# Half of a first layer by seven chained half-size products, with its sums, orders and stores rearranged

## The chip, the core and the metric

The kernel runs on one core of a Trainium2 chip. The core has TensorE (PE in the profile: matrix products into PSUM, with weight loads as PEld), VectorE (DVE), ScalarE (ACT), GpSimd (POOL), and DMA queues that are issued from SyncE (SP), ScalarE or GpSimd. Each engine works through its own instructions in the order in which the program lists them, and waits where an operand of another engine isn't there yet. SBUF is the working memory, PSUM the small memory that only TensorE accumulates in and that ScalarE and VectorE read and write; this kernel uses it as four pairs of banks, each pair 128 partitions x 2 x 448 floats. The metric is the time of one execution on the device in microseconds (us). The profile is one such execution, recorded by the hardware; its span runs from the first to the last instruction.

## What is computed

An attention with normalised q and k, 8 batches of 12 heads, 448 tokens and 64 dimensions, and behind it two layers over 3584 tokens (d_model 768, d_ff 2048) with a gelu between them:

```python
q_n, k_n = rmsnorm(q, g_q), rmsnorm(k, g_k)
attn = softmax(q_n @ k_n^T / sqrt(64))
x = (attn @ v) as 3584 tokens x 768
h = x @ w_in                                  # 768 x 2048
g = 0.5*h*(1 + tanh(sqrt(2/pi)*(h + 0.044715*h**3)))
out = g @ w_out                               # 2048 x 768
```

## The kernel before

The order of every engine's work is written out by hand (a manual schedule). For batch b the kernel runs `attention(b)` (line 584) and then the first layer of b, in the loop at line 1009. Inside `attention(b)` TensorE interleaves, by the strings `STEADY` and `SECOND`, the scores of 21 units (`unit`), the row sums and products with v (`products`), and the second layer of the batch before (`quartered`). ScalarE does the exps; VectorE adds the exps up (steps A, B, F, G), transposes and inverts the sums (`turned`, `recip`, `spread`: T, R, S) and writes x, transposed, as `xT[b]` (`quad_x`: M).

The **first layer** of b multiplies the six 128-row chunks of `xT[b]` (448 tokens wide) with `win`, 2048 columns in 16 blocks of 128. Two blocks make one PSUM pair, so there are eight pairs, and behind each ScalarE writes `g` by one gelu of 128 x 896. From batch 1 on each product is cut into quarters of 64 x 64 (`mm1_turn`, line 523, products at line 537): four of them, on different quarters of the array, make one 128x128 product. Chunks 4 and 5 of x come last from the attention; so the first pairs are begun with chunks 0 to 3 (`early`, at the end of `attention`) and finished in the loop at line 1076 (`late`).

Beside the first layer of b, by the entries of `m1` (step of the loop, action), run: on GpSimd the normalisation of the next batch's q and k (`normed_both`, three chunks, line 278) and some squares for the batch after that (`square`), held back at first by a small copy that waits for VectorE (`gpsimd_waits`); on SP's queue the transposing DMAs of the normalised q and k (`transposed`) and loads for the batch after (`loads`); on ScalarE the other half squares (`squared`, line 162); on VectorE their sums (`total`, line 173) and the gain of k (`gain`, line 325), which waits for the transposing DMA. Entries under "first" in `extra` come at the start of the next attention.

The **second layer** works with two batches' `g` side by side. Only its last 512 tokens, behind batch 7, are done in `final` (line 728) by seven products of half size (Strassen's scheme in Winograd's form, TensorE at line 754), from sums of `w_out` (`weight_sum`, line 717) and of tokens of `g` (`token_sums`, lines 723 to 726) that VectorE makes beside batch 7's first layer. `put_out` stores results by two DMAs for each piece, both from SP's queue, but for the very last pieces, where ScalarE's queue takes one of the two.

The PSUM pairs are handed out in turn by `pair`. Buffers: `xT` has two, `ex` (exps of a chunk, 128 x 6272 bf16) two, the stage results `st` and `rb` of VectorE one each.

Of the kernel before, what the change touches and what calls it, by code (L numbers as in the profile page):

```python
# [17 lines left out]
def kernel(  # L18
# [38 lines left out]
    xp = ctx.enter_context(tc.tile_pool(name="xp", bufs=2))  # L57
# [346 lines left out]
    def spread(rs=slice(0, 2), rc=None):  # L404
        m = S // 32
        if rs.start == 0:
            oas["rb"] = stp.tile([128, 2, S], F32, tag="rb", name="rb")
# [159 lines left out]

    early, late = range(HP - 2), range(HP - 2, HP)
# [15 lines left out]
    def attention(b, side, extra, ends):  # L584
# [94 lines left out]
        mm1_turn(b, 0, 0, early, begin=True)  # L679
        mm1_turn(b, 1, 0, early, begin=True)  # L680
        mm1_turn(b, 0, 1, early)
        if b == 1:
            mm1_turn(b, 2, 0, early, begin=True)
        mm1_turn(b, 1, 1, early)
        if b == 1:
            mm1_turn(b, 2, 1, early)
# [10 lines left out]
    def sums_homes():  # L697

        two = exq.tile([P, 2 * NJ, HD], BF16, tag="ex", name="tw")
        one = exq.tile([P, NJ, HD], BF16, tag="ex", name="tw")  # L700
        sw.update({3: two[:, :NJ], 2: two[:, NJ:], 4: one})
        sw[1] = w4[:, :, 0, HD:]

        def home(t):
            return t[:, :NJ * TH].rearrange("p (j s) -> p j s", j=NJ)

        sa[1] = g4[:, :, 0, late2]
        sa[2] = home(kT.rearrange("p c t r s -> p (c t r s)"))
        sa[3] = home(vb[0].rearrange("p h t d -> p (h t d)"))
        sa[4] = home(vb[1].rearrange("p h t d -> p (h t d)"))  # L710

    def weight_sum(i):
# [3 lines left out]
        x, y = {3: (b12, b22), 2: (b11, sw[3]), 4: (b21, sw[2]), 1: (b12, b11)}[i]  # L716
        nc.vector.tensor_sub(sw[i], x, y)
# [10 lines left out]
    def final(b):  # L728

        token_sums(slice(NJ - 2, NJ))  # L730
        tiles = [[op.tile([128, d_model], F32, tag="osb", name="osb") for _ in range(2)]]
# [6 lines left out]
        def operands(i, j, t):  # L738
# [4 lines left out]
            if i == 4:  # L743
                return g4[:, j, 1, late2.start + lo:late2.start + lo + 128], sw[4][:, j]
# [24 lines left out]
        for t in range(2):  # L769
# [13 lines left out]
            for lo in (0, HD // 2):  # L783
                cols = slice(HD + lo, HD + lo + HD // 2)
                add(c1[:, cols], product(3, t, lo, lo + HD // 2), c1[:, cols])
                put_out(t, 0, cols, (nc.sync, nc.scalar))
# [222 lines left out]
    for b in range(B):  # L1009
        m1, side, extra, ends = [], [], [], []  # L1010
        if b == 0:
# [10 lines left out]
            extra += [("first", lambda: late_loads(2, 0)), ("L0", lambda: late_transposed(1, 2)),  # L1022
# [15 lines left out]
        elif b + 1 < B:  # L1038

            m1.append((0, lambda: gpsimd_waits(ess[b, NCH - 1][:1, 0, 0, :1])))  # L1040
            if b == 1:
                halves = [(n, slice(a, a + 1)) for n in "qk" for a in range(2)]
                m1 += [(0, lambda n=n, hs=hs: square(2, 1, n, nc.gpsimd, hs)) for n, hs in halves]
                m1 += [(0, lambda n=n, hs=hs: total(2, 1, n, hs)) for n, hs in halves]
                m1 += [(0, lambda n=n: total(2, 2, n)) for n in "qk"]
                m1.append((0, lambda: rsqrt_last(2, slice(1, NCH))))
            for c in range(NCH):
                m1 += [(0, lambda c=c: normed_both(b + 1, c, nc.gpsimd)),
                       (4 * c + 4, lambda c=c: turns_and_loads() if (b, c) == (1, 1)
                        else transposed(b + 1, c))]  # L1050
            m1.append((9, lambda: gain(b + 1, 0)))
            if b == 1:
                extra.append(("first", lambda: gain(2, 1)))
            else:
                m1.append((14, lambda: gain(b + 1, 1)))
        if 0 < b and b + 2 < B:
            m1.append((4, lambda: loads(b + 2, 1)))
            if b > 1:
                m1.append((8, lambda: loads(b + 2, 2)))
            for c, at in ((0, 4), (1, 9)):  # L1060
                for i, (n, a) in enumerate((n, a) for n in "qk" for a in range(2)):
                    m1.append((at + i, lambda c=c, n=n, a=a: squared(b + 2, c, n, a)))
                m1 += [(at + 2, lambda c=c: total(b + 2, c, "q")),
                       (at + 4, lambda c=c: total(b + 2, c, "k"))]
            for n in "qk":
                m1.append((13, lambda n=n: square(b + 2, 2, n, nc.gpsimd)))
                extra.append(("first", lambda n=n: total(b + 2, 2, n)))
        if 0 < b and b + 1 < B:
            extra.append(("first", lambda: gain(b + 1, 2)))
        if b + 1 == B:  # L1070
            m1.append((4, sums_homes))
            m1 += [(f, lambda i=i: weight_sum(i)) for f, i in ((4, 3), (6, 2), (8, 4), (10, 1))]
            m1 += [(f, lambda js=js: token_sums(js))
                   for f, js in ((7, slice(0, 4)), (11, slice(4, 6)))]
        m1 = plan(*m1)
        for f in range(nf // 2 if b == 0 else nf):
# [72 lines left out]
```

## Time and profile before

| | us |
|---|---|
| median of 3 runs | 389.36 (388.61 to 389.49) |
| the profiled execution | 389.53 |
| its span | 387.8 |
| first layers of batches 1 to 7 (line 537), busy | 128.7 |
| second layers (line 495), busy | 152.0 |
| scores (line 335), busy | 59.9 |
| exps on ScalarE (line 343), busy | 156.1 |
| gelus on ScalarE (line 543), busy | 50.5 |
| seven products at the end (line 754), 128 of TensorE's instructions | 364.7 to 383.1 |

Times in the trace count from the start of the span. A row of a timeline gives start, duration, engine, line, operation, written tile <- read tiles, shape, the number of instructions merged into it (x33), and in brackets how long the engine was idle before and for whom it waited. A row of the groups gives, behind the count, the busy time in us and the mean of one instruction in ns, then the idle time before. A row of the chain gives start, duration and what. Recorded products on TensorE overlap: the next one starts before the end of the one before, so the distance of their starts is what a product costs.

### The profile page before, as it was taken

The numbers are of one execution on the slowest core, as the hardware profiler recorded it, in microseconds if no ns is written. First come the engines' busy times: TensorE is split into PE (matmuls) and PEld (weight loads), VectorE is DVE, ScalarE is ACT, GpSimd is POOL, SyncE is SP. The second block draws the span as 40 slices with busy tenths as digits, with TensorE's granted clock in tenths as the row PEclk, the third lists the DMA queues.
The fourth block names the chain that finished last, engine by engine and source line by source line (L and its number), as shares of the span: only waits on it lengthen the run. The fifth ranks groups of instructions, "written<-read, shape, count | busy, mean of one in ns | idle before, by whom it ended". The sixth has DMA issues, their size and how long they took to land.

```text
span 387.8 us, 17506 instructions
## 1 busy us (share of the span) xinstructions
PE 379.0 (98%) x8020; PEld 294.2 (76%) x8020; DVE 259.9 (67%) x394; ACT 276.6 (71%) x348; POOL 126.0 (33%) x109
## 2 busy tenths in 40 slices
PE   8899999999999999999999999999999999999995
PEld 5565586679888788877888778877888778887653
DVE  5998949984896259835589156963588503895743
ACT  6995599677994689757996589946897449953400
POOL 5996504448105440083102740064400810000000
PEclk9999999999999999999999999999999999999999
DMA  8999999979914992369822995159823630220033
GB/s 274 318 232 210 210 227 230 263 176 181 222 44 99 258 199 55 85 139 224 176 73 64 181 257 110 45 111 235 111 61 82 109 59 19 69 64 5 2 79 83
DMA packets 65085, 54.66 MB, mean 141 GB/s; under 512 B 37748, under 2 KB 61172, under 8 KB 65012
## 3 DMA queue, kind: packets, MB, share of 16 engines
q1 hardware_dynamic: 54576, 41.43, 44.5%
q0 software_dynamic: 10128, 11.80, 18.4%
q8 instruction: 62, 1.02, 1.0%
q10 hardware_dynamic: 308, 0.33, 0.3%
q14 instruction: 11, 0.09, 0.1%
HBM read 45.61 MB, written 11.01 MB: 146 GB/s over the span
## 4 chain that ended last, share of the span: by engine, by line
PE 92%; ACT 5%; DMA 1%; issue 1%; DVE 0%; POOL 0%
PE t L537 33%; PE t L495 32%; PE t L387 9%; PE t L335 8%; PE t L754 5%; ACT ex L343 4%; PE t L556 4%; DMA rawq<-in_q_dram 1%; PE h L436 1%; PE tp L296 1%; PE o L387 0%; POOL nrmq L278 0%; DVE ss L173 0%; ACT sq L162 0%; PE os L387 0%
## 5 line engine op out<-in xcount | busy, mean ns | idle before, releaser
L343 ACT ACTIVATE ex<-t,shift 128x896 bf16<-128x896 f32 x168 | 156.1, 1012 | 3.0 <-PE t L335 2.6
L495 PE MATMUL t<-wout,g 64*64 64x384 bf16 (+1 forms) x3456 | 152.0, 305 | 0.0
L495 PEld LDWEIGHTS <-g 64*64 64x64 bf16 x3456 | 115.4, 107 | 17.6 <-issue 0.2
L537 PE MATMUL t<-xT,win 64*64 64x448 bf16 x2688 | 128.7, 349 | 0.0
L537 PEld LDWEIGHTS <-win 64*64 64x64 bf16 x2688 | 98.0, 107 | 29.2
L543 ACT ACTIVATE g<-t 128x896 bf16<-128x896 f32 x56 | 50.5, 915 | 56.8 <-PE t L537 56.7
L173 DVE TENSOR_REDUCE ss<-sq 128x14 f32<-128x896 f32 (+3 forms) x45 | 44.3, 998 | 49.4 <-ACT sq L162 47.0
L335 PE MATMUL t<-qT,kT 64*64 64x448 bf16 x672 | 59.9, 351 | 1.5 <-ACT ex L343 0.6
L876 POOL COPY mark<-es 1x1 bf16<-1x1 bf16 x7 | 1.2, 177 | 134.8 <-DVE es L362 126.4
L355 DVE TENSOR_TENSOR es<-ex 128x1792 bf16<-128x1792 bf16 x21 | 22.3, 1061 | 28.9 <-ACT ex L343 28.9
L278 POOL TENSOR_TENSOR nrmq<-rawq,rinv 128x896 bf16<-128x896 f32 (+1 forms) x21 | 34.8, 1658 | 19.5 <-ACT rinv L205 10.5
L278 POOL TENSOR_TENSOR nrmk<-rawk,rinv 128x896 bf16<-128x896 f32 (+1 forms) x21 | 34.6, 1647 | 0.0
L387 PE MATMUL t<-ex,vb 64*64 64x448 bf16 x588 | 32.4, 350 | 0.5 <-issue 0.5
L335 PEld LDWEIGHTS <-kT 64*64 64x64 bf16 x672 | 26.2, 106 | 8.0 <-issue 1.9
L397 DVE STREAM_TRANSPOSE st<-t 128x448 f32<-128x448 f32 x42 | 24.7, 627 | 9.6 <-PE t L387 9.6
L387 PEld LDWEIGHTS <-vb 64*64 64x64 bf16 x672 | 23.2, 107 | 8.6 <-issue 2.1
L409 DVE STREAM_TRANSPOSE rb<-rc 128x896 f32<-128x896 f32 (+1 forms) x25 | 26.7, 1068 | 0.3
L422 DVE TENSOR_TENSOR xT<-t,rb 128x896 bf16<-128x896 f32 x21 | 22.8, 1086 | 0.9 <-PE t L387 0.2
L513 ACT COPY osb<-t 128x768 f32<-128x768 f32 (+1 forms) x18 | 12.6, 701 | 14.0 <-PE t L495 14.0
L358 DVE TENSOR_TENSOR es<-es,ex 128x1792 bf16<-128x1792 bf16 x21 | 22.3, 1062 | 0.0
L164 POOL TENSOR_TENSOR sq<-rawq 128x896 f32<-128x896 f32 (+1 forms) x9 | 13.6, 1510 | 24.3 <-DVE ss L173 11.6
L325 DVE TENSOR_SCALAR kT<-kT,gcols 128x896 bf16<-128x896 bf16 x19 | 12.1, 639 | 11.2 <-DMA kT<-nrmk 11.2
(122 smaller groups left out, 322.5 us busy)
## 6 DMA issues: line engine op xcount, KB each, us to landing
rawq<-in_q_dram SPq DMA_DIRECT2D x22, 448.0 KB, 4.6
rawk<-in_k_dram SPq DMA_DIRECT2D x22, 448.0 KB, 6.3
out_dram<-osb SPq DMA_DIRECT2D x36, 192.0 KB, 2.8
vb<-in_v_dram POOLq DMA_DIRECT2D x6, 672.0 KB, 8.1
out_dram<-osb SPq DMA_DIRECT2D x38, 96.0 KB, 2.2
win<-in_moe_w_in_dram POOLq DMA_DIRECT2D x8, 384.0 KB, 10.4
wout<-in_moe_w_out_dram POOLq DMA_DIRECT2D x3, 768.0 KB, 17.2
vb<-in_v_dram POOLq DMA_DIRECT2D x2, 448.0 KB, 15.2
```

The lines of the kernel that those rows point to most:

```text
L173: nc.vector.reduce_sum(sss[b][:, seat(b, c), "qk".index(n), hs, ts], squares(b, c, n, hs, ts), axis=AX.X)
L278: eng.tensor_mul(nrms[n, b, c][:, ts].rearrange("p t a d -> p a t d"), raws[n, b, c][:, :, ts], root[:, :, ts].to_broadcast([P, 2, m, D]),)
L335: nc.tensor.matmul(sc[r * R:(r + 1) * R, a, :S], kT[rs, c, t, r], qT[b][rs, c, :, r], start=True, stop=True,)
L343: nc.scalar.activation(exs[b, c][:, t], scs.pop((b, c, t))[:, :, :S], AF.Exp, scale=scale, bias=shift)
L355: nc.vector.tensor_add(es, ex[:, :2], ex[:, 2:4])
L387: nc.tensor.matmul(o[r][a * D:(a + 1) * D], vb[b % 2][rs, 2 * c + a, i] if what else ones[rs], es[i][rs, a], start=(i == 0), stop=(i == n ...
L397: nc.vector.transpose(st[:, r].rearrange("p a b -> p (a b)"), o[r])
L409: nc.vector.transpose(oas["rb"][:, rs].rearrange("p r s -> p (r s)"), rc.to_broadcast([128, (rs.stop - rs.start) * m, 32]),)
L422: nc.vector.tensor_mul(xT[b][:, 2 * c:2 * c + 2], oas["o", c, 1][:, :, :S], oas["rb"])
L495: mm = nc.tensor.matmul(o[a * R:(a + 1) * R, bank, :hi - lo], g[rs, f, at:at + R], wout[rs, f, lo:hi], start=(n == 0), stop=(n == len(step ...
L537: mm = nc.tensor.matmul(h[a * R:(a + 1) * R, j, :S], win[rs, c, at:at + R], xT[b][rs, c], start=begin and c == cs[0], stop=end and c == cs ...
L543: nc.scalar.activation(g[:, 2 * i:2 * i + 2, (b % 2) * S:(b % 2 + 1) * S], h[:, :, :S], AF.Gelu_apprx_tanh,)
```

## The change

For batches 2 to 7 the first layer is written anew (class `Seven`). Blocks 4 to 7 and 12 to 15 of d_ff (pairs 2, 3, 6 and 7, `LONE`) are multiplied in whole 128x128 products of 448 columns. Blocks 0 to 3 and 8 to 11 (two halves of 512 columns of `win`), chunks 0, 2, 4 against 1, 3, 5, and the two halves of the tokens (224 each) are the quadrants of Strassen's scheme: seven products, each of 4 blocks x 3 chunks in whole 128x128 products of 224 columns. They are chained in three PSUM pairs: X takes products 1, 6, 7 and 4 one upon the other, Z products 5 and 3, Y product 2. ScalarE copies X to SBUF (`keep`) after 1, after 6 and after 7, and VectorE adds the copies to Y and Z. VectorE makes four sums of x (`x_sums`, 128 x 672 bf16) in each batch. The sums of `win` are made once: three at the start of attention 1 (`in_sums`, into a new tile `wx`), one in place at the start of attention 2.

```diff
+    FS, QS = 4, S // 2
+    wv = win.rearrange("p (m k) f -> p k m f", k=2)
+    wx = wts.tile([128, 3, NCH, FS * 128], BF16, name="wx")
+    fs1, fs2 = slice(0, FS * 128), slice(d_ff // 2, d_ff // 2 + FS * 128)
+    LONE = (2, 3, 6, 7)
+    def in_sums():
+        a11, a21, a12, a22 = wv[:, 0, :, fs1], wv[:, 0, :, fs2], wv[:, 1, :, fs1], wv[:, 1, :, fs2]
+        nc.vector.tensor_sub(wx[:, 1], a21, a11)
+        nc.vector.tensor_add(wx[:, 0], wx[:, 1], a22)
+        nc.vector.tensor_sub(wx[:, 2], a12, wx[:, 0])
+    def in_place_sum():
+        a21 = wv[:, 0, :, fs2]
+        nc.vector.tensor_add(a21, a21, wv[:, 1, :, fs2])
+    class Seven:
...
+            self.rhs = {1: b11, 2: b21, 3: b22, 4: xs[:, 3], 5: xs[:, 2], 6: xs[:, 1], 7: xs[:, 0]}
+            self.lhs = {1: wv[:, 0, :, fs1], 2: wv[:, 1, :, fs1], 4: wv[:, 1, :, fs2],
+                        5: wv[:, 0, :, fs2], 6: wx[:, 0], 7: wx[:, 1], 3: wx[:, 2]}
+        def x_sums(self):
+            b11, b12, b21, b22 = self.given
+            xs, sub = self.xs, nc.vector.tensor_sub
+            sub(xs[:, 0], b12, b22)
+            sub(xs[:, 1], b11, xs[:, 0])
+            sub(xs[:, 2], b12, b11)
+            sub(xs[:, 3], b21, xs[:, 1])
...
+        def keep(self, n):
+            nc.scalar.copy(self.snaps[n], self.of("X"))
...
+        def early(self):
+            hs1.clear()
+            two = range(NCH - 1)
+            self.lone(LONE[0], range(2), early)
+            self.product(1, "X", two)
+            self.product(2, "Y", two)
+        def rest(self, steps):
...
+            self.x_sums()
+            side(0)
+            product(1, "X", one)
+            self.keep(0)
+            product(2, "Y", one)
+            add(self.of("Y"), self.of("Y"), self.snaps[0])
+            lone(LONE[0], range(2), late, end=True)
+            side(1)
+            product(6, "X")
+            self.keep(1)
+            self.gelu(self.of("Y"), 0, 0)
+            side(2)
+            product(5, "Z")
+            side(5)
+            product(7, "X")
+            self.keep(0)
+            add(self.snaps[0], self.of("Z"), self.snaps[0])
+            side(8)
+            lone(LONE[1], ones_, all_of)
+            self.gelu(self.snaps[0], 1, 1)
+            product(4, "X")
+            self.gelu(self.of("X"), 1, 0)
+            side(11)
+            product(3, "Z")
+            add(self.of("Z"), self.of("Z"), self.snaps[1])
+            self.gelu(self.of("Z"), 0, 1)
+            lone(LONE[1], twos, all_of, end=True)
+            side(15)
+            lone(LONE[2], range(2), all_of, end=True)
+            side(17)
+            lone(LONE[3], range(2), all_of, end=True)
```

The work beside the first layers of batches 2 to 6 gets new places (`side(n)` runs the entries of step n). GpSimd normalises chunk 0, then waits for the last sum of x, then goes on. ScalarE keeps six of the eight half squares, GpSimd takes the other two as one whole:

```diff
+            m1 += [(0, lambda: gpsimd_waits(ess[b, NCH - 1][:1, 0, 0, :1])),
+                   (0, lambda: normed_both(b + 1, 0, nc.gpsimd)),
+                   (0, lambda: gpsimd_waits(sevens[b].xs[:1, 3, 0, :1])),
+                   (0, lambda: normed_both(b + 1, 1, nc.gpsimd)),
+                   (0, lambda: normed_both(b + 1, 2, nc.gpsimd)),
+                   (2, lambda: transposed(b + 1, 0)), (8, lambda: transposed(b + 1, 1)),
+                   (11, lambda: transposed(b + 1, 2))]
+            if b + 2 < B:
+                m1 += [(0, lambda n=n, a=a: squared(b + 2, 0, n, a))
+                       for n in "qk" for a in range(2)]
+                m1 += [(2, lambda: loads(b + 2, 1)), (8, lambda: loads(b + 2, 2))]
+                m1 += [(5, lambda n=n: total(b + 2, 0, n)) for n in "qk"]
+                m1 += [(15, lambda a=a: squared(b + 2, 1, "q", a)) for a in range(2)]
+                m1.append((15, lambda: square(b + 2, 1, "k", nc.gpsimd)))
+                m1 += [(17, lambda n=n: total(b + 2, 1, n)) for n in "qk"]
...
+            m1 += [(5, lambda: gain(b + 1, 0)), (17, lambda: gain(b + 1, 1))]
             extra.append(("first", lambda: gain(b + 1, 2)))
+            m1 += [(5, sums_homes), (5, lambda: weight_sum(3)), (5, lambda: weight_sum(2)),
+                   (11, lambda: weight_sum(4)), (17, lambda: token_sums(slice(2, 6))),
+                   (17, lambda: token_sums(slice(0, 2)))]
```

Memory for it: `xT` has one buffer, `rb` shares that of `st`, the sums of x and the two copies of X lie in a buffer of `ex`, and one sum of `w_out` moves to two buffers of the raw q and k. At the end, the last sum of `w_out` (`weight_sum(1)`) is made in `final` behind the last token sums, and the stores are joined: a row of tiles goes out whole, half from SP's queue and half from ScalarE's, and so does the very last half row:

```diff
             add(c2[:, last], p5, c2[:, first])
             add(c1[:, last], p5, c1[:, last])
-            put_out(t, 1, last)
             add(c2[:, first], product(4, t), c2[:, first])
-            put_out(t, 1, first)
+            put_out(t, 1, slice(0, d_model), (nc.sync, nc.scalar))
...
                 add(c1[:, cols], product(3, t, lo, lo + HD // 2), c1[:, cols])
-                put_out(t, 0, cols, (nc.sync, nc.scalar))
+            put_out(t, 0, last, (nc.sync, nc.scalar))
```

More of the change, by code (lines that the diff above doesn't have):

```diff
@@ L568 @@
+    sevens = {}
     early, late = range(HP - 2), range(HP - 2, HP)
@@ L678, in attention @@
                 square(2, NCH - 1, m, nc.scalar)
[L679 to L682, printed above, removed]
+        if b > 1:
+            sevens[b] = Seven(b)
+            sevens[b].early()
+        else:
+            mm1_turn(b, 0, 0, early, begin=True)
+            mm1_turn(b, 1, 0, early, begin=True)
+            mm1_turn(b, 0, 1, early)
             mm1_turn(b, 2, 0, early, begin=True)
-        mm1_turn(b, 1, 1, early)
-        if b == 1:
+            mm1_turn(b, 1, 1, early)
             mm1_turn(b, 2, 1, early)
@@ L1037 @@
                     (f"a{at}", lambda n=n: total(2, 0, n))]
-        elif b + 1 < B:
+        elif b == 1:
             m1.append((0, lambda: gpsimd_waits(ess[b, NCH - 1][:1, 0, 0, :1])))
[L1041 to L1046, printed above, removed]
-            for c in range(NCH):
[L1048 to L1059, printed above, removed]
+            halves = [(n, slice(a, a + 1)) for n in "qk" for a in range(2)]
+            m1 += [(0, lambda n=n, hs=hs: square(2, 1, n, nc.gpsimd, hs)) for n, hs in halves]
+            m1 += [(0, lambda n=n, hs=hs: total(2, 1, n, hs)) for n, hs in halves]
+            m1 += [(0, lambda n=n: total(2, 2, n)) for n in "qk"]
+            m1.append((0, lambda: rsqrt_last(2, slice(1, NCH))))
@@ L1068 @@
-        if 0 < b and b + 1 < B:
-            extra.append(("first", lambda: gain(b + 1, 2)))
[L1070 to L1074, printed above, removed]
+                m1.append((13, lambda n=n: square(3, 2, n, nc.gpsimd)))
+                extra.append(("first", lambda n=n: total(3, 2, n)))
@@ L1075 @@
         m1 = plan(*m1)
-        for f in range(nf // 2 if b == 0 else nf):
+        if b > 1:
+            sevens[b].rest(m1)
+        for f in range((nf // 2, nf)[b] if b < 2 else 0):
             i, part = f // 4 * 2, f % 4
```

106 lines of the change are left out of this document (95 added, 11 removed).

## The prediction

> **What bounds the kernel now.** I read the page first, then the chain of waits in order of time, then the groups of instructions with shapes kept apart, then the timeline around one first layer, and last the DMA queue at the end.
>
> ```profile
> span 387.8 us, 17506 instructions
> PE 379.0 (98%) x8020; PEld 294.2 (76%) x8020; DVE 259.9 (67%) x394; ACT 276.6 (71%) x348; POOL 126.0 (33%) x109
> PE 92%; ACT 5%; DMA 1%; issue 1%; DVE 0%; POOL 0%
> ```
>
> TensorE is busy for 98% of the span, and the chain that ended last runs 92% through it. ScalarE and VectorE have about 30% to spare, but a busy share alone doesn't say whether they are idle at the right moment. The chain of waits has the stage that the change rewrites (here in batches 3 and 7, then the last products):
>
> ```profile
> 211.07 18.16 PE t L537 x384
> 346.60 18.16 PE t L537 x384
> 364.76 18.34 PE t L754 x120
> ```
>
> A first layer of a late batch is one unbroken piece of 18.16 us. It holds 384 quarter products, four of which do the work of one whole 128x128 product: 96 whole ones at 18.16 / 96 = 0.189 us. Nothing waits in it, so work removed there is time removed, unless the new order adds waits.
>
> **The products.** How far apart do whole 128x128 products start? The timeline has all widths but the new one:
>
> ```profile
> 39.78 6.41 PE L556 MATMUL t<-xT,win 128*128 128x448 bf16 x33
> 380.31 1.46 PE L754 MATMUL t<-tw,g 128*128 128x384 bf16 x8
> 381.61 1.48 PE L754 MATMUL t<-wout,vb 128*128 128x192 bf16 x16
> L754 PE MATMUL t<-wout,vb 128*128 128x192 bf16 x16 | 1.5, 246 | 0.0
> L754 PEld LDWEIGHTS <-g 128*128 128x128 bf16 x64 | 6.1, 98 | 4.4 <-issue 0.4 <-ACT g L543 0.2
> L537 PEld LDWEIGHTS <-win 64*64 64x64 bf16 x2688 | 98.0, 107 | 29.2
> ```
>
> At 448 columns: (6.41 - 0.35) / 32 = 0.189 us, the same as four quarters. At 384: (381.61 - 380.31) / 8 = 0.1625. At 192: (1.48 - 0.246) / 15 = 0.0823. The slope is (0.1625 - 0.0823) / 192 = 0.000418 us a column, so 224 columns, which no row shows, cost 0.0823 + 32 x 0.000418 = 0.0957; the bounds are 0.0823 and, should a weight load be the limit, 0.098 (that of a whole block) or 0.107 (the longest row of loads from win); I take the line between the widths shown. New stage: half of d_ff stays ordinary, 4 pairs x 2 x 6 = 48 products of 448 columns, 48 x 0.1892 = 9.08 us. The other half is seven products of 4 blocks x 3 chunks, 84 of 224 columns (96 without Strassen), 84 x 0.0957 = 8.04 us. Together 17.12, which is **1.04 us less** than 18.16, in six batches **6.24 us**.
>
> The Trainium skill, page "TensorE: Matmul & The Clock Gate", section "LDWEIGHTS (loading the stationary operand)", puts a weight load at its columns divided by 1.2, an estimate of 107 ns for 128. By that rule the 84 products would be held to their loads, and the stage would gain almost nothing (rival C has the mechanism by rows). The trace speaks against it: products of 192 columns follow each other every 82 ns, each with a load of its own that is recorded at 98 ns, so loads overlap there.
>
> **The waits that the chain adds.** Seven products share three PSUM pairs: X collects products 1, 6, 7, 4 and is copied out by ScalarE three times on the way, Y is product 2, Z products 5 and 3. TensorE, in order, must wait for each copy before it adds to X again, and everything behind it on its queue waits too. The prices:
>
> ```profile
> 18.37 9.12 ACT ex L343 x10
> 27.54 0.38 PE t L335 x4
> 229.28 0.92 ACT L543 ACTIVATE g<-t 128x896 bf16<-128x896 f32 x1 [0.22 <-PE t L537]
> L513 ACT COPY osb<-t 128x768 f32<-128x768 f32 x12 | 9.7, 812 | 0.0
> L513 ACT COPY osb<-t 128x384 f32<-128x384 f32 x6 | 2.9, 478 | 14.0 <-PE t L495 14.0
> L774 DVE TENSOR_TENSOR osb<-t,osb 128x384 f32<-128x384 f32 x2 | 1.1, 558 | 1.5 <-PE t L754 1.5
> L422 DVE TENSOR_TENSOR xT<-t,rb 128x896 bf16<-128x896 f32 x21 | 22.8, 1086 | 0.9 <-PE t L387 0.2
> ```
>
> ScalarE starts 0.05 us after the recorded end of a product (211.07 + 18.16 = 229.23), that end lies 0.246 - 0.082 = 0.16 us behind its slot, and TensorE restarts 0.05 us after ScalarE. A copy of 896 columns isn't shown: the two copies give (812 - 478) / 384 = 0.87 ns a column, so 0.92 us, between 0.81 and some 1.01 (an exp of that shape). From the end of a product's slot to the next use of X: 0.16 + 0.05 + 0.92 + 0.05 = 1.18 us. What stands between as cover: product 2's last chunk and four ordinary products before product 6 (0.38 + 0.76 = 1.14), product 5 before 7 (12 x 0.0957 = 1.15), half a pair before 4 (6 x 0.189 = 1.14). Each is short by about 0.04. Product 3 needs VectorE's add of Z behind the third copy (1.09 us by the nearest row): 1.18 + 0.05 + 1.09 = 2.32 against 1.14 + 0.04 + 1.15 = 2.33. So 0.1 us a stage if ScalarE and VectorE are free on the dot; I take **0.15 x 6 = 0.9 us**, bounds 0 and 0.6 a stage.
>
> Are they free? These rows of the timeline and the groups answer it:
>
> ```profile
> 210.87 18.36 PE L537 MATMUL t<-xT,win 64*64 64x448 bf16 x384
> 210.86 1.28 ACT L675 ACT_TABLE_LOAD   x1
> 224.42 1.03 ACT L162 ACTIVATE sq<-rawq 128x448 f32<-128x448 f32 x2
> 212.27 1.09 DVE L422 TENSOR_TENSOR xT<-t,rb 128x896 bf16<-128x896 f32 x1
> 212.64 1.68 POOL L278 TENSOR_TENSOR nrmk<-rawk,rinv 128x896 bf16<-128x896 f32 x1
> 99.55 0.44 DVE L325 TENSOR_SCALAR kT<-kT,gcols 128x896 bf16<-128x896 bf16 x1
> 87.28 1.69 POOL L278 TENSOR_TENSOR nrmk<-rawk,rinv 128x896 bf16<-128x896 f32 x1
> 88.23 0.99 DVE L325 TENSOR_SCALAR kT<-kT,gcols 128x896 bf16<-128x896 bf16 x1
> 308.03 2.01 DVE L325 TENSOR_SCALAR kT<-kT,gcols 128x896 bf16<-128x896 bf16 x1 [4.13 <-DMA kT<-nrmk]
> 308.11 1.68 POOL L278 TENSOR_TENSOR nrmq<-rawq,rinv 128x896 bf16<-128x896 f32 x1
> L360 DVE TENSOR_TENSOR es<-es 128x896 bf16<-128x896 bf16 x20 | 12.5, 624 | 0.7
> L173 DVE TENSOR_REDUCE ss<-sq 128x14 f32<-128x896 f32 x37 | 39.9, 1082 | 45.8 <-ACT sq L162 43.5 <-POOL sq L164 2.3
> ```
>
> In stage time, with zero at 210.87, where the first product starts, ScalarE's table load ends at 1.3, four half squares (two take 1.03) end at 3.4, and the first copy is due at 3.6. The gelus of the ordinary half fall between the copies, 0.92 us each. VectorE's order is where it may go wrong. The gain of k takes 0.44 us alone (at 99.55); begun beside a GpSimd product it ends only 0.25 us after that product (88.23 + 0.99 = 89.22, the product ends at 88.97), and begun at 308.03, less than 0.1 us before GpSimd goes on to its next at 308.11, it waits for that one too (2.01 us). The last chunks of x are there at 2.49. The four sums of x, some 0.5 us each, end at 4.45, or near 5.25 if they too are held by the GpSimd product that ends at 3.45. Either way product 6, due at 4.6, finds its sum (the second) at 4.35 at the latest. Then come in order the add of Y (1.09), two totals (1.08 each) and gain 0, which arrives at 7.8, or 8.5 if the sums were held, and must be done by 9.2, when the add for product 3 is due. GpSimd, which now waits for the sums, multiplies back to back from about 4.6, or 5.45, 1.68 each: boundaries at 8.0 and 9.6, or 8.8 and 10.5. In either order gain 0 passes at the first of the two and is done by 9.05, in time; I take that, and it is close.
>
> On this the Trainium skill, page "GPSIMD Engine Reference", section "8. Key points", says that GpSimd contends with VectorE in 2-port modes and with two SBUF inputs. The gain's rows agree for the first kind; for the second, which the sums of x are, no run shows it.
>
> **Edits at the edges.** Rows of the groups and of the timeline:
>
> ```profile
> 55.24 1.09 DVE L355 TENSOR_TENSOR es<-ex 128x1792 bf16<-128x1792 bf16 x1 [4.35 <-ACT ex L343]
> L726 DVE TENSOR_TENSOR vb<-g,kT 128x1024 bf16<-128x1024 bf16 x1 | 0.7, 685 | 0.0
> 100.25 1.09 DVE L355 TENSOR_TENSOR es<-ex 128x1792 bf16<-128x1792 bf16 x1 [0.27 <-ACT ex L343]
> 103.97 0.63 DVE L362 TENSOR_TENSOR es<-es,ex 128x896 bf16<-128x896 bf16 x1
> 104.65 0.45 PE L387 MATMUL t<-es,ones 64*64 64x448 bf16 x4
> 235.24 1.09 DVE L355 TENSOR_TENSOR es<-ex 128x1792 bf16<-128x1792 bf16 x1 [3.56 <-ACT ex L343]
> ```
>
> Sums of w_in, 1536 columns: between 0.69 (1024) and 1.06 (1792), I take 0.93. Three stand at the start of the attention of batch 1, before the first add of exps, where VectorE idles 4.35 us: hidden, 2.8 < 4.35. The in-place one stands at the start of batch 2's attention, where only 0.27 us is idle behind gain 2: the adds begin 0.55 us later, and the row sums that TensorE does 0.05 us after the last of them (104.60 to 104.65) come late by as much. **+0.5 us**, bounds 0 and 0.7. In later attentions the squares and totals that now end the stage run perhaps 1.7 us into the 3.56 us of idle time before the first add: hidden.
>
> Batch 7: two of the sums of w_out (1.75 each, by rows of 3072 columns) end at about 9.2, again just where the add for product 3 is due; the sums of tokens and the last of w_out end some 2 us into the final products, and TensorE needs a PSUM pair from the adds behind them 0.6 us later. Counted at nothing, within the 0.6 a stage.
>
> The last stores:
>
> ```profile
> 383.13 0.36 DVE L785 TENSOR_TENSOR osb<-t,osb 128x192 f32<-128x192 f32 x1 [0.30 <-PE t L754]
> 383.59 1.42 SPq L456 DMA_DIRECT2D out_dram<-osb  x2
> 384.44 0.56 SPq L456 DMA_DIRECT2D out_dram<-osb  x1
> ```
>
> The last add ends at 383.49, but SP's queue issues its last store at 384.44. With one store less ahead, and the rest shared with ScalarE's queue, the last goes out near 383.55: 0.9 us sooner. It is twice as large (64 rows of 384 floats, 96 KB) and behind two of 192 KB that leave 1.2 us before it: **-0.5 us**, bounds 0 and -0.9.
>
> Sharing a buffer between st and rb, and one xT in place of two, cost nothing: VectorE writes and reads both in order, and the first layer is over before the next xT.
>
> **Sum** against the profiled execution's 389.53 us: -6.24 + 0.9 + 0.5 - 0.5 = -5.34, 384.2. The median of the runs, 389.36, lies 0.17 lower; from there **384.0 us**. A difference of 0.2%, 0.8 us, is about what a measurement of this kernel can tell from none.
>
> **The rivals.** (A) The covers are shorter than the chain: a copy that takes 1.01 us, a gain 0 that passes one boundary late in the order in which the sums aren't held (9.6 + 0.25, so product 3 late by 0.7). That is 0.3 to 0.7 us a stage more, 386 to 388, say 387.0. For it: all four covers are equal to the need within 0.05 us. Against: nothing else stands on ScalarE at those moments.
> (B) Slower: in the held order gain 0 comes to VectorE after the boundary at 8.8 and waits to 10.5 + 0.25; the add then ends at 11.85 and product 3 starts 1.5 us late, in each of the four stages that have totals (batches 2 to 5): +6.2, **390.2 us**. It decides once VectorE's queue is 0.3 us later than worked out. For it: the row of 2.01 us. Against: its arrival leaves those 0.3 us.
> (C) Weight loads hold the narrow products at the 107 ns that loads from win show: 84 x 0.107 + 9.08 = 18.07 a stage, 6 x 0.09 gained instead of 6.24, which with 0.9 of waits gives 389.7. Against: the 192-column row, 82 ns apart.
> (D) No wait shows, the whole 0.9 us is had at the end and the in-place sum is absorbed: 389.36 - 6.24 - 0.9 = 382.2.
>
> **How the numbers follow.** Forecast 0.62 (382.6 to 385.6 by its own bounds), A 0.20, B 0.07, C 0.03, D 0.08. Faster: forecast, A and D, less 0.02 of A's tail: 0.88. Same: C and that tail, 0.05. Slower: B, 0.07. The range 382.4 to 387.6 takes in the forecast, most of A and part of D, and leaves out B, C and the rest.
>
> **What would show it.** 84 products of 224 columns 96 ns apart; stages of 17.2 to 17.4 us in the chain; TensorE's idle time at lines of the seven products, put to the copy or the add, below 0.1 us each; gain 0 in batches 2 to 5 no longer than about 0.7 us; a stall of 0.5 us at batch 2's first row sums; the last store issued within 0.1 us of the last add. Idle time of over 0.5 us before product 3 would make it wrong (A, B), as would narrow products over 100 ns apart (C).

## The result and the profile after

The changed kernel takes 384.65 us (median of 4 runs, 384.31 to 384.90) against 389.38 (4 runs, 388.61 to 389.49) beside it: a ratio of 0.9882, with a 95% interval of 0.9865 to 0.9899. That is 4.73 us less, where the prediction has 5.34 less. Its profiled execution took 384.59 us, 4.94 below the one of before. Its span is 382.8 us. The engines' busy times from its page, and the shares of the chain of waits:

```profile
PE 374.9 (98%) x6508; PEld 273.6 (71%) x6508; DVE 299.4 (78%) x441; ACT 289.6 (76%) x358; POOL 134.1 (35%) x118
PE 92%; ACT 5%; DMA 1%; DVE 0%; issue 0%; POOL 0%
```

TensorE is still the bound, busy for 98% of a span that is 5.0 us shorter. VectorE does 39.5 us more than before and is hardly in the chain. One rewritten first layer, that of batch 4 (the one that ran at 211.07 before; the prediction calls it batch 3), from the chain of waits, its first and last piece:

```profile
209.78 1.62 PE t L652 x8
...
221.44 5.67 PE t L652 x30
```

L652 are the ordinary products, L625 those of the seven. From the first start to the last end it is 17.33 us (221.44 + 5.67 - 209.78), where 18.16 stood. From the start of this stage to that of the next it is 44.33 us (209.78 to 254.11), where it was 45.00 (211.07 to 256.07): 0.67 less a stage. The timeline of TensorE shows the starts, and with them the gaps:

```profile
208.26 1.52 PE L387 MATMUL t<-ex,vb 64*64 64x448 bf16 x28
209.72 1.69 PE L652 MATMUL t<-xT,win 128*128 128x448 bf16 x8
211.24 2.46 PE L625 MATMUL t<-xT,win 128*128 128x224 bf16 x24
213.54 0.92 PE L652 MATMUL t<-xT,win 128*128 128x448 bf16 x4
214.31 1.31 PE L625 MATMUL t<-xs,wx 128*128 128x224 bf16 x12
...
216.62 1.31 PE L625 MATMUL t<-xs,wx 128*128 128x224 bf16 x12
217.76 1.30 PE L652 MATMUL t<-xT,win 128*128 128x448 bf16 x6
218.98 1.31 PE L625 MATMUL t<-xs,win 128*128 128x224 bf16 x12
220.12 1.31 PE L625 MATMUL t<-xT,wx 128*128 128x224 bf16 x12
221.27 5.84 PE L652 MATMUL t<-xT,win 128*128 128x448 bf16 x30
227.04 1.01 PE L495 MATMUL t<-wout,g 64*64 64x384 bf16 x20
```

Take each row's start and count, and see whether the next row starts on time. The 24 narrow products at 211.24 take 2.30, 0.0957 each. The four late ordinary ones (4 x 0.189 from 213.54) end at 214.30, product 6 (L625 at 214.31) starts 0.01 late; product 7, two times 12 x 0.0957 later, at 216.62, again 0.01 late; the six of half a pair end their slots at 217.76 + 6 x 0.189 = 218.89, product 4 starts at 218.98, 0.085 late; product 3 at 220.12 is on time. The prediction named no more than this. But there are two further gaps: the 28 quarter products at 208.26 (seven slots of 0.189) end at 209.585 and the first whole product comes at 209.72, **0.135 late**; the last 30 whole ones end at 226.95 and the next quarter product comes at 227.04, **0.09 late**. Nothing is waited for there, as the weight loads of the same places show:

```profile
209.71 1.25 PEld L652 LDWEIGHTS <-win 128*128 128x128 bf16 x8 [0.36 <-issue]
...
227.04 0.63 PEld L495 LDWEIGHTS <-g 64*64 64x64 bf16 x20 [0.37 <-issue]
```

Elsewhere in the stage the next load starts ahead of its product, while the product before it still runs (at 211.05 for the product at 211.24); at these two places the load path is idle for 0.36 us, and the next load starts only with its product.

The side work of the same stage, from the timelines of VectorE, GpSimd and ScalarE:

```profile
211.29 1.68 POOL L278 TENSOR_TENSOR nrmk<-rawk,rinv 128x896 bf16<-128x896 f32 x1
212.29 1.05 DVE L610 TENSOR_TENSOR xs<-xT 128x672 bf16<-128x672 bf16 x1
213.38 0.51 DVE L611 TENSOR_TENSOR xs<-xT,xs 128x672 bf16<-128x672 bf16 x1
215.66 0.91 ACT L636 COPY xs<-t 128x896 f32<-128x896 f32 x1 [0.25 <-PE t L625]
216.64 1.68 POOL L278 TENSOR_TENSOR nrmk<-rawk,rinv 128x896 bf16<-128x896 f32 x1
217.63 0.94 DVE L325 TENSOR_SCALAR kT<-kT,gcols 128x896 bf16<-128x896 bf16 x1
218.96 1.09 DVE L695 TENSOR_TENSOR xs<-t,xs 128x896 f32<-128x896 f32 x1 [0.39 <-ACT xs L636]
```

The first sum of x (L610) takes 1.05 us where the next takes 0.51: it ends at 213.34, 0.37 after the GpSimd product beside it (212.97). So the first sum was held, which is the second of the two orders in the prediction. Gain 0 (L325) begins at 217.63, ends at 218.57, 0.25 behind the end of GpSimd's product, and VectorE is idle for 0.39 us before the add that product 3 needs.

### The profile page after: what moved, and what is told of

It reads as the page before. It is cut to its first block, busy times and chain, and to the rows that moved or that the text cites. A ratio compares the mean times of both kernels' runs of the same rounds, so it can differ in the third digit from the quotient of the medians.

```text
span 382.8 us, 14538 instructions
## 1 busy us (share of the span) xinstructions
PE 374.9 (98%) x6508; PEld 273.6 (71%) x6508; DVE 299.4 (78%) x441; ACT 289.6 (76%) x358; POOL 134.1 (35%) x118
## 4 chain that ended last, share of the span: by engine, by line
PE 92%; ACT 5%; DMA 1%; DVE 0%; issue 0%; POOL 0%
PE t L495 33%; PE t L652 14%; PE t L625 13%; PE t L387 9%; PE t L335 8%; PE t L537 5%; PE t L914 5%; ACT ex L343 4%; PE t L556 4%; DMA rawq<-in_q_dram 1%; PE h L436 1%; PE tp L296 1%; PE o L387 0%; DVE ss L173 0%; POOL nrmq L278 0%
## 5 line engine op out<-in xcount | busy, mean ns | idle before, releaser
L495 PEld LDWEIGHTS <-g 64*64 64x64 bf16 x3456 | 104.4, 107 | 29.2 <-issue 2.2
L335 PE MATMUL t<-qT,kT 64*64 64x448 bf16 x672 | 57.5, 351 | 1.4 <-ACT ex L343 0.6
L652 PE MATMUL t<-xT,win 128*128 128x448 bf16 x288 | 58.5, 353 | 0.0
L173 DVE TENSOR_REDUCE ss<-sq 128x14 f32<-128x896 f32 (+3 forms) x45 | 43.5, 995 | 18.5 <-ACT sq L162 16.1
L652 PEld LDWEIGHTS <-win 128*128 128x128 bf16 x288 | 27.7, 98 | 24.1 <-issue 2.1
L335 PEld LDWEIGHTS <-kT 64*64 64x64 bf16 x672 | 23.7, 106 | 9.4 <-issue 1.4
L625 PEld LDWEIGHTS <-win 128*128 128x128 bf16 x288 | 27.6, 98 | 2.7 <-issue 1.0
L658 ACT ACTIVATE g<-t 128x896 bf16<-128x896 f32 x24 | 22.0, 916 | 9.3 <-PE t L652 9.3
L636 ACT COPY xs<-t 128x896 f32<-128x896 f32 x18 | 16.3, 906 | 13.0 <-PE t L625 10.5
L164 POOL TENSOR_TENSOR sq<-rawk 128x896 f32<-128x896 f32 (+1 forms) x14 | 22.6, 1614 | 0.7 <-DMA rawk<-in_k_dram 0.7
## 6 DMA issues: line engine op xcount, KB each, us to landing
win<-in_moe_w_in_dram POOLq DMA_DIRECT2D x8, 384.0 KB, 11.6
```

The source lines that it names most:

```text
L164: eng.tensor_mul(sq, raw, raw)
L173: nc.vector.reduce_sum(sss[b][:, seat(b, c), "qk".index(n), hs, ts], squares(b, c, n, hs, ts), axis=AX.X)
L335: nc.tensor.matmul(sc[r * R:(r + 1) * R, a, :S], kT[rs, c, t, r], qT[b][rs, c, :, r], start=True, stop=True,)
L495: mm = nc.tensor.matmul(o[a * R:(a + 1) * R, bank, :hi - lo], g[rs, f, at:at + R], wout[rs, f, lo:hi], start=(n == 0), stop=(n == len(step ...
L625: nc.tensor.matmul(t[:, bank, n * QS:(n + 1) * QS], self.lhs[i][:, m, at:at + 128], self.rhs[i][:, m], start=i == owner and n == m == 0, s ...
L652: nc.tensor.matmul(h[:, j, :S], win[:, c, at:at + 128], xT[self.b][:, c], start=(c == 0), stop=(c == HP - 1),)
```

## The experiments

The experiments were run on three chips, each time with the kernel before beside them: 389.31 us (the experiments on switches and the first on rival B), 389.46 and 389.38. On the second and third chip the changed kernel itself was run again, and these two are what its variants are compared with; on the first it was not:

> The changed kernel itself, beside the others on the same chip: 384.65 within 0.3.

> The changed kernel beside these three on the same chip: 384.65 within 0.5.

They gave 385.18 (384.74 to 386.75, ratio 0.9893, 0.9872 to 0.9914) and 385.06 (384.18 to 385.45, ratio 0.9892, 0.9872 to 0.9911). So 4.3 to 4.7 us are saved, and variants are read against about 385.1.

### What does a switch of product size cost?

The kernel before has whole 128x128 products only in its first batch and its last layer. In the first experiment it gets them in the first layers of batches 2 to 7 too, without Strassen: the same 18.16 us of products by the rate of the two kinds, but with a switch of size at both ends of each stage.

```diff
     def mm1_turn(...):
+        if b > 1:
...
+            at = (2 * i + turn) * 128
+            for c in cs:
+                nc.tensor.matmul(
+                    hs1[i][:, turn, :S], win[:, c, at:at + 128], xT[b][:, c],
...
```

> The kernel before, with the first layers of batches 2 to 7 in whole 128x128 products of 448 columns in place of quarters; no Strassen. Theory (a switch between quarter and whole products drains the array): products still 0.189 us apart, but 0.13 us lost where a stage starts and 0.09 us where it ends, 6 x 0.22 = 1.3 us more than the 389.4 of before, about 390.7. Rival (the 0.2 us a stage belongs to the chain of seven): no change, 389.4.

It took 390.64 us (389.96 to 392.54), ratio 1.0042 (1.0025 to 1.006): 1.33 more than before. The same stage in the timeline of TensorE:

```profile
212.10 1.52 PE L387 MATMUL t<-ex,vb 64*64 64x448 bf16 x28
213.56 18.33 PE L532 MATMUL t<-xT,win 128*128 128x448 bf16 x96
231.82 1.01 PE L495 MATMUL t<-wout,g 64*64 64x384 bf16 x20
```

212.10 + 7 x 0.189 = 213.42, so 0.14 at the entry; 213.56 + 96 x 0.1892 = 231.72, so 0.10 at the exit. Six entries and five exits are 1.3 us; batch 7 now goes on to the whole products of the last layer without a switch, and so saves the one that stood there. That makes a sum of 1.2, and the result is 0.1 above it (the interval of the ratio reaches from 1.0 to 2.3 us). The switch alone, with no chain, no copy and no sum, costs what the changed kernel's stages were short of.

Two more experiments put one pair of the ordinary half back into quarters, inside the stage or at its end:

```diff
-            lone(LONE[2], range(2), all_of, end=True)
+            mm1_turn(self.b, LONE[2], 0, range(HP), begin=True)
+            mm1_turn(self.b, LONE[2], 1, range(HP), end=True)
```

> The changed kernel, with the ordinary pair 6 (LONE[2]) of batches 2 to 7 in quarter products between whole ones. Theory (each switch costs): two more switches in a stage, 6 x 0.22 = 1.3 us more than 384.65, about 386.0, and idle time of about 0.1 us on either side of that pair. Rival (the gaps belong to the edges of a stage): 384.65.

> The changed kernel, with the last ordinary pair (LONE[3]) of batches 2 to 7 in quarter products, so that the switch back to quarters comes ahead of it and not at the end of the stage. Theory (each switch costs, wherever it is): as many switches, 384.65 within 0.3. Rival (the gap at the end belongs to the start of the attention): the gap stays and another comes, 6 x 0.09 = 0.5 us more, 385.2.

(The second does the same with LONE[3].) They took 388.49 (ratio 0.9975, 0.9959 to 0.999) and 387.12 (0.9942, 0.9922 to 0.9962), both longer than either theory allowed. The timeline of TensorE of the first of them:

```profile
221.93 1.30 PE L652 MATMUL t<-xT,win 128*128 128x448 bf16 x6
223.16 2.73 PE L537 MATMUL t<-xT,win 64*64 64x448 bf16 x48
225.82 2.44 PE L652 MATMUL t<-xT,win 128*128 128x448 bf16 x12
```

The switch in costs 223.16 - (221.93 + 6 x 0.189) = 0.10. But the pair of 48 quarters takes 2.66 instead of 2.27. A weight load in the midst of it waits for TensorE's own products:

```profile
224.56 0.90 PEld L537 LDWEIGHTS <-win 64*64 64x64 bf16 x24 [0.50 <-PE t L537]
```

The two turns of a pair add to the same places in PSUM, and the code makes the second wait for the first's last product (`follows` in `mm1_turn`). Before puts a turn of another pair between the two, and no such wait showed there; here they come one right behind the other. In the timeline of the second, the pair at the end lasts 225.79 to 228.35, 2.56 us, 0.29 more than its slots, and no gap follows it:

```profile
222.29 3.57 PE L652 MATMUL t<-xT,win 128*128 128x448 bf16 x18
225.79 2.73 PE L537 MATMUL t<-xT,win 64*64 64x448 bf16 x48
228.35 0.98 PE L495 MATMUL t<-wout,g 64*64 64x384 bf16 x20
```

222.29 + 18 x 0.189 = 225.69: the 0.10 moved from the stage's exit to the pair's entry, and 6 x 0.29 = 1.7 is most of the 2.0 by which it lies above 385.1. In the first, 0.29 for the turns and two switches of 0.10 make 0.5 a stage, 3.0 of its 3.4. So the gaps follow each switch, as the theory has it; the totals were missed through a wait that the edit brought in. That this wait makes the 0.29 is read from the traces; a run with another pair's turn in between was not made.

### How near was VectorE to the cliff of rival B?

The change lets GpSimd wait for the sums of x. Without that:

```diff
-                   (0, lambda: gpsimd_waits(sevens[b].xs[:1, 3, 0, :1])),
```

> The changed kernel, without the small copy by which GpSimd waits for the last sum of x in batches 2 to 6. Theory (VectorE's operations on two SBUF operands are held by a running GpSimd product, and each of the four finds a new one running): the second sum ends some 0.8 us after product 6 is due, the third and fourth a GpSimd product (1.65 us) later each, product 3 late by 2 to 3.5 us a stage: 394 to 401 us. Rival (only the first sum was slow, for a reason of its own): GpSimd starts its next chunk 1.7 us sooner, 384.65 within 0.6.

401.22 us (400.86 to 402.15), ratio 1.031 (1.0282 to 1.0338). The timelines of VectorE and GpSimd:

```profile
219.51 1.04 DVE L610 TENSOR_TENSOR xs<-xT 128x672 bf16<-128x672 bf16 x1
220.16 1.95 POOL L278 TENSOR_TENSOR nrmq<-rawq,rinv 128x896 bf16<-128x896 f32 x1
220.59 1.88 DVE L611 TENSOR_TENSOR xs<-xT,xs 128x672 bf16<-128x672 bf16 x1
222.07 1.95 POOL L278 TENSOR_TENSOR nrmk<-rawk,rinv 128x896 bf16<-128x896 f32 x1
222.39 1.99 DVE L612 TENSOR_TENSOR xs<-xT 128x672 bf16<-128x672 bf16 x1
```

Each sum and each GpSimd product now take turns: 1.9 to 2.0 us for a sum that takes 0.51 alone. TensorE waits for them:

```profile
222.53 1.32 PE L625 MATMUL t<-xs,wx 128*128 128x224 bf16 x12 [0.85 <-DVE xs L611]
224.43 1.31 PE L625 MATMUL t<-xs,win 128*128 128x224 bf16 x12 [0.58 <-DVE xs L612]
...
229.10 1.31 PE L625 MATMUL t<-xs,win 128*128 128x224 bf16 x12 [1.07 <-ACT xs L636]
230.69 1.31 PE L625 MATMUL t<-xT,wx 128*128 128x224 bf16 x12 [0.28 <-DVE xs L695]
```

The brackets add up to 2.8 us in this stage, and the starts, counted in slots as above, to about 3.4; five such stages (batches 2 to 6) make the 16 us. The Trainium skill, page "SBUF — State Buffer", section "SBUF: two separate sides", describes a port pair that VectorE and GpSimd lock for a whole instruction, among others by a VectorE operation with two SBUF inputs while GpSimd reads SBUF; the other engine then blocks entirely. The trace agrees: 0.51 becomes 1.05 beside one product and 1.9 between two.

That is not rival B itself. B needs VectorE to come to gain 0 too late. The next run lays one more total (about 1.08 us, its result not needed) ahead of gain 0; the one after it does the same and moves gain 0 three steps back, behind the add for product 3's copy:

```diff
-                m1 += [(5, lambda n=n: total(b + 2, 0, n)) for n in "qk"]
+                m1 += [(5, lambda n=n: total(b + 2, 0, n)) for n in "qkk"]
...
-            m1 += [(5, lambda: gain(b + 1, 0)), (17, lambda: gain(b + 1, 1))]
+            m1 += [(8, lambda: gain(b + 1, 0)), (17, lambda: gain(b + 1, 1))]
```

(The first has only the upper edit.)

> The changed kernel, with one total (1.04 us of VectorE, the same result again) more ahead of gain 0 in batches 2 to 5. Theory (the hold makes a cliff): gain 0 arrives 0.4 us behind the end of a GpSimd product, waits for the next one and ends 0.25 us after it, the add behind it ends 1.2 us late for product 3: 4 x 1.2 = 4.9 us more, 389.5. Rival (VectorE's queue alone): gain 0 ends after 0.44 us, product 3 is late by 0.15: 385.2.

> The same with one total more, but gain 0 moved from step 5 to step 8, behind the add of Z. Theory (hold): the totals end 0.2 us before the add is due, and gain 0 is held where nobody waits: 384.65 within 0.3. Rival (the queue's length is what counts): as with gain 0 in step 5.

389.50 us (389.01 to 391.25), ratio 1.0005 (0.9991 to 1.0018): the whole gain is lost. With the gain late as well: 384.80 (384.6 to 385.34), ratio 0.9881 (0.9862 to 0.99), with the same extra work on VectorE. The timelines of the first:

```profile
220.82 1.68 POOL L278 TENSOR_TENSOR nrmq<-rawq,rinv 128x896 bf16<-128x896 f32 x1
221.28 1.47 DVE L325 TENSOR_SCALAR kT<-kT,gcols 128x896 bf16<-128x896 bf16 x1
222.67 1.08 DVE L695 TENSOR_TENSOR xs<-t,xs 128x896 f32<-128x896 f32 x1
223.80 1.31 PE L625 MATMUL t<-xT,wx 128*128 128x224 bf16 x12 [0.99 <-DVE xs L695]
```

Gain 0 comes 1.08 later, finds the next GpSimd product running, ends 0.25 behind it (222.75), and the add with all that follows is late. Product 4 started at 221.50, so product 3 was due at 222.65 and is 1.15 late; in the four stages that have totals, 4.6 us, where the medians show 4.3. The cause is the place of the gain in VectorE's order, not the amount of work: in the run with the gain moved, gain 0 is held for even longer (1.89 us from 220.66), but behind the add, and product 3 starts on time (12 slots behind product 4: 219.67 and 220.81).

### How much room has the sum in place?

One of the sums of w_in is made once more, from the same operands into the same place, ahead of the one in place at the start of attention 2:

```diff
     def in_place_sum():
+        nc.vector.tensor_sub(wx[:, 2], wv[:, 1, :, fs1], wx[:, 0])
         a21 = wv[:, 0, :, fs2]
```

> The changed kernel, with one sum of w_in (0.94 us of VectorE, the same result again) more ahead of the in-place sum at the start of attention 2. Theory (the in-place sum used up the slack there to the last 0.05 us): the row sums come late by 0.9 us, 385.55. Rival (there is slack left, as in the later attentions): 384.65.

386.42 us (385.75 to 387.26), ratio 0.9921 (0.9903 to 0.9939): 1.24 above the changed kernel beside it, though the two intervals overlap. The prediction expected the row sums of this attention to come late by 0.5. These are the attention's first scores and its row sums in the changed kernel and, below, in this run (timelines of TensorE):

```profile
94.72 0.39 PE L335 MATMUL t<-qT,kT 64*64 64x448 bf16 x4
104.72 0.38 PE L387 MATMUL t<-es,ones 64*64 64x448 bf16 x4
```

```profile
95.57 0.47 PE L335 MATMUL t<-qT,kT 64*64 64x448 bf16 x4
106.22 0.38 PE L387 MATMUL t<-es,ones 64*64 64x448 bf16 x4
```

Times from the start of the span don't compare here. This execution comes to the attention 0.85 us later already, with TensorE idle for 1.09 us at 73.40, before the first layer of batch 1, where the edit changes nothing; that idle time differs between executions of one kernel as well (none in the changed kernel's first profile, 1.58 us in its second). Counted from the first scores, the row sums begin after 9.88 us in the kernel before, after 10.00 in the changed kernel (10.13 and 9.86 in its two repeats), and after 10.65 in this run. So a second sum delays them by 0.5 to 0.8 of its own 0.94 us, and there is little room behind the one sum that stands there. How much of the 1.24 this makes is open: from the start of batch 1's first layer to that of batch 2's this run takes 45.96 us, the changed kernel 45.45 to 45.59 in its three profiles, which is 0.4 to 0.5 less. Why the one sum cost next to nothing needs another reason, below.

### The short cover of product 4, and the stores

Product 4 is the only one that waits visibly (0.085 us a stage). Here the other half of the ordinary pair is moved ahead of it:

```diff
             lone(LONE[1], ones_, all_of)
+            lone(LONE[1], twos, all_of, end=True)
             self.gelu(self.snaps[0], 1, 1)
             product(4, "X")
...
-            lone(LONE[1], twos, all_of, end=True)
             side(15)
```

> The changed kernel, with the second half of the ordinary pair 3 (LONE[1]) moved ahead of product 4, so that twelve ordinary products and not six cover the third copy of X. Theory (the copy chain is 0.085 us longer than its cover there): product 4 starts without a wait, 6 x 0.085 = 0.5 us less than the changed kernel. Rival (the wait comes back at pair 6, whose PSUM pair the gelu of X now frees later): no change within 0.2.

387.04 us (386.51 to 387.9), ratio 0.9945 (0.9927 to 0.9963), 2.0 more than the changed kernel beside it: a miss for both theories, though the place is the rival's. The timelines of TensorE and ScalarE:

```profile
221.24 1.31 PE L625 MATMUL t<-xs,win 128*128 128x224 bf16 x12
222.15 0.90 ACT L658 ACTIVATE g<-t 128x896 bf16<-128x896 f32 x1
222.39 1.31 PE L625 MATMUL t<-xT,wx 128*128 128x224 bf16 x12
222.94 0.91 ACT L640 ACTIVATE g<-t 128x896 bf16<-128x896 f32 x1
223.91 4.70 PE L652 MATMUL t<-xT,win 128*128 128x448 bf16 x24 [0.20 <-ACT g L640]
```

Product 4's wait has gone: it starts at 221.24, where the twelve ordinary products before it (from 218.97) end. But the next ordinary pair needs the PSUM pair of X, whose gelu now stands behind the gelu of the pair that was moved: 222.39 + 1.15 = 223.54, and it starts 0.37 late. 6 x (0.37 - 0.085) = 1.7 of the 2.0. The half pair that stood behind product 3 had been the cover of this gelu.

The same with gain 0 moved back as well:

> Both rearrangements: pair 3 whole ahead of product 4, and gain 0 in step 8. Theory: as with pair 3 alone, 0.5 us less than the changed kernel, and no hold of gain 0 ahead of the add of Z. Rival: no change within 0.2.

387.00 us, ratio 0.9939 (0.9918 to 0.9959): the same; the gain is not what waits here.

Last, the old stores in the new kernel:

```diff
+            put_out(t, 1, last)
...
-            put_out(t, 1, slice(0, d_model), (nc.sync, nc.scalar))
+            put_out(t, 1, first)
...
-            put_out(t, 0, last, (nc.sync, nc.scalar))
+                put_out(t, 0, cols, (nc.sync, nc.scalar))
```

> The changed kernel with the last stores as before (each half row by itself, the final half in two). Theory (SP's queue issues its last store 0.6 to 0.9 us later): from the last add to the end 4.3 us as before and not 4.0, so 0.3 us more than the changed kernel. Rival (the landing of the large last store is what counts): no change.

385.05 us (384.63 to 385.55), ratio 0.9891 (0.987 to 0.9911), against 385.06. In the traces the time from the end of the last add to the end of the span is 0.2 us shorter with the joined stores (378.39 to 382.4, against 378.58 to 382.8), but the medians don't show it.

## Why the prediction held, step by step

**The rate of narrow products: right.** 0.0957 was worked out between two widths, and 0.0957 was measured. Rival C is out: each of these products has a load of its own, recorded at 98 ns, and they follow each other faster than the 107 ns of the loads from win before. The 1.04 us a stage was had.

**The waits of the chain: right, on the small side.** Product 6 0.01, product 7 0.01, product 4 0.085, product 3 none: 0.1 us a stage where 0.15 was taken. The copy took 0.91 (0.92 estimated from two other copies), the add 1.09. Rival A didn't come about, since ScalarE was free on the dot each time.

**VectorE's order: right, with more room than it said.** Of the two orders, the held one came, by the row of 1.05 us; the bound on a VectorE sum beside a GpSimd product, which no row of before showed, had been taken from the gain's rows, and it fits (0.37 behind the product, 0.25 for the gain). Gain 0 passed at the first boundary, 0.39 us ahead of need, though it took 0.94 us where the prediction allowed about 0.7. The prediction put rival B's point at 0.3 us. By the trace, gain 0 began 0.66 us before GpSimd went on to its next product (217.63 against 218.29), so the margin is an estimated 0.6 to 0.7. A delay of 1.08 us brought rival B about in full, at 389.50 where 390.2 was worked out; no smaller one was tried.

**What was left out: the switches of size.** The saving was forecast from rates inside stages of one kind. Before, each late stage was quarters between quarters, with one switch into the last layer; after, whole products stand between quarters, and each stage loses 0.135 at its entry and 0.09 at its exit (at batch 7 only the entry). With the switch that goes at the end, this is 6 x 0.135 + 5 x 0.09 - 0.135 = 1.1 us, and the first experiment measured 1.33 for the same switches. It is the largest term that was missing. A stage then gains 1.04 - 0.1 - 0.225 = 0.715 us, and the distance of the stages' starts shows 0.67. The row was at hand: in before's timeline batch 7 starts at 346.41, 96 products of 0.189 end at 364.57, and the whole products come at 364.70, 0.13 late:

```profile
346.41 18.36 PE L537 MATMUL t<-xT,win 64*64 64x448 bf16 x384
364.70 2.61 PE L754 MATMUL t<-wout,g 128*128 128x384 bf16 x15
```

The Trainium skill, page "TensorEngine Tiling (Array Packing)", section "Key Properties", says that a change of the tiling mode drains TensorE, without a figure; the trace agrees, with 0.09 to 0.14 us.

**The sum in place: costed at +0.5, and next to nothing came of it.** The work did take its 0.94 us in the place named, but gain 2 ahead of it came sooner: counted from the attention's first scores (94.77 before, 94.72 after) it began after 4.78 us before and after 4.38 in the changed kernel, and the row sums came 0.12 late. GpSimd's last square, ahead of gain 2, waits for its load in both kernels (timeline of GpSimd, before and then after):

```profile
95.71 1.68 POOL L164 TENSOR_TENSOR sq<-rawk 128x896 f32<-128x896 f32 x1 [1.66 <-DMA rawk<-in_k_dram]
```

```profile
95.26 1.68 POOL L164 TENSOR_TENSOR sq<-rawk 128x896 f32<-128x896 f32 x1 [0.71 <-DMA rawk<-in_k_dram]
```

Counted the same way, the load landed 0.4 us sooner. That needn't be the change's doing: in the first experiment, which has no such sum and the side work of before, the same square began at 96.63, even ahead of the first scores at 96.85, and gain 2 after 3.62 us (100.47). So the 0.27 us of slack on which the prediction built belonged to one execution in which a load came late, not to the kernel. It can come out the other way too: in the profiled execution of the run with pair 3 ahead of product 4, a transposing DMA was late, gain 2 began after 5.27 us, and the row sums came after 10.89 us instead of 9.88. This term is a matter of when transfers land, and the prediction's lower bound of 0 was the right one here.

**The tail: right in sign, smaller.** The last store was issued as forecast, 0.02 us behind the last add (378.83 against 378.81), where it had been 0.95 behind. But from the last add's end to the span's end it took 3.99 us (378.81 to 382.8) instead of 4.31: of 0.9 us in the issue only 0.3 arrived at the end, where -0.5 was taken. And the experiment on the stores finds no difference that the medians show. Of rival D, then, one part came, the absorbed sum; the waits and the tail were those of the forecast, only smaller.

**The sum again.** -6.2 for products, +0.6 for waits, +1.1 for switches, 0 for the sum in place, -0.3 for the tail: -4.8. The spans differ by 5.0. About 0.5 of that is a stumble that, of these two executions, only before's has, in one attention, where TensorE's next load comes 0.58 us late (at 283.90) and waits for nothing that the profile shows. So the account closes to about 0.3 us. The forecast of 384.0 was 0.65 below the measured 384.65: the missing 1.1 of switches was made up in part by 0.5 for a sum that cost next to nothing and by 0.3 of waits that were not there, while 0.2 of the tail went the other way. The products, the waits and VectorE's order were right in their mechanism; that the total came out nearer than its terms is luck.

## What to carry to other kernels

Count the boundaries, not only the products: where one kind of product is replaced by another between neighbours of the old kind, each stage pays for two switches, and the price can be read where the kernel already has one. A chain through a second engine is free if the cover in front of each link is as long as the link, but a cover belongs to everyone behind it in the queues: take it for one wait and look whose gelu or PSUM pair it had been covering. Where VectorE shares work with GpSimd, what decides is which VectorE operation meets a running GpSimd product, and moving one operation behind the urgent add bought back the whole loss that 1.08 us of extra work had caused. And a slack of 0.3 us read from one execution, where a transfer ends the wait, is not a property of the kernel: read it in several.

## What the chip showed that was not expected

A switch costs TensorE 0.14 us from quarter to whole products at a stage's start (some 0.10 in the midst of one) and 0.09 to 0.10 back, though the rates on both sides are the same; loads don't run ahead across it (idle for 0.36 us).

Beside a GpSimd product of 1.68 us, a VectorE sum of 0.51 us ends 0.37 us after the product, and where GpSimd has products in a row the two engines alternate, 1.9 to 2.0 us a sum. Over the kernel this made 16 us out of one wait left out in each of five batches.

One operation of 1.08 us on VectorE, an engine that is idle for a fifth of the span, cost 4.3 us (389.50 against 385.18), and moving the gain behind the add that TensorE waits for gave all of it back.
